# Linear attention into channel mix on one core: q and v loads dealt out anew, one batch turned by TensorE, three by VectorE, a new order

## The chip, the core and the metric

The kernel runs on one core of one Trainium2 chip. The metric is device time in microseconds of one execution; the median of three executions counts. The engines are TensorE (PE, its weight loads PEld), VectorE (DVE), ScalarE (ACT), GpSimd (POOL) and SyncE (SP); SP, ACT and POOL also issue DMAs.

## What is computed

Two stages, one behind the other. For 4 batches of 4 heads, 1088 tokens and head size 32, q and k are projected on two sketches of 8 rows; the outer product of the two projections (64 features) stands in for the softmax. The result, seen as 1088 x 128 for each batch, goes through a token shift and a squared-ReLU mix with a hidden size of 1024.

```python
def phi(x):
    a = np.einsum('rd,bhsd->bhsr', S1, x)
    b = np.einsum('rd,bhsd->bhsr', S2, x)
    return np.einsum('bhsi,bhsj->bhsij', a, b).reshape(*x.shape[:-1], r * r)
q_p, k_p = (phi(q), phi(k))
kv = np.einsum('bhsf,bhsd->bhfd', k_p, v)
z = np.sum(k_p, axis=2)
num = np.einsum('bhsf,bhfd->bhsd', q_p, kv)
den = np.einsum('bhsf,bhf->bhs', q_p, z)[..., None] + 1e-06
attn_out = num / den
...
x = np.ascontiguousarray(attn_out.transpose(0, 2, 1, 3)).reshape(B, S, H * D)
...
xk = mu_k * x + (1.0 - mu_k) * x_prev
xr = mu_r * x + (1.0 - mu_r) * x_prev
k = np.maximum(xk @ w_k, 0.0)
v = k * k @ w_v
r = 1.0 / (1.0 + np.exp(-(xr @ w_r)))
return r * v
```

## The kernel before

Everything stays in on-chip memory between the stages. The program is a list of small tasks, written out by hand in the string `ORDER`: each entry is a function's name, its numbers (a batch, a half or a group), the engine (A, V, G, S for ACT, DVE, POOL, SP) and, behind @, the banks of PSUM that it writes. Each engine runs its own instructions in exactly that order and waits at an instruction until what it needs is there. `LOADS` lists the input loads and the engine that issues each, in the same way (`k01@S` is the second piece of batch 0's k, issued by SP; w0, w1, w2 are the three weights); eight semaphores (called DMAHW0 to DMAHW7) are shared out among the DMAs of SP and ACT, and a DMA that takes a semaphore again waits until the DMA that had it has landed.

The tasks of the attention of a batch b, in the order of need:

- `kturn` (DVE, two halves) transposes k in blocks of 32; `kproj` (PE) projects it; `abev` copies the projections out of PSUM (tile `ab`), and `kp` multiplies them to features.
- `zmm`, `zev`, `wmm`, `wsq` sum the features of k, send the sum back through the sketch and put it beside the query's sketch (tile `SQ`), so that one product with q gives the features and the denominator together.
- `qturn` (DVE) transposes q, `abw` (PE) projects it with `SQ`, `abwev` copies it out; `pw`, `dred`, `drec` make the reciprocal of the denominator, `an` scales one factor with it, `qp` (DVE) forms the query's 64 features.
- `kvmm` (PE) forms the state from `kp` and v, `kvev`, `kdmm`, `kvcp` bring it into place.
- The query's features must be transposed once more before they meet the state. The set `TURNED` says how: a batch in it is turned by TensorE (`qtt`, `qt`: 17 transposes through PSUM, copied out by `qttev` and `qtev`, then `xt` and `xmh`), the others by one block transpose of VectorE (`qf`), followed by `xmm` with 32 x 32 tiles of the array.
- `xev`, `xtev` copy the result out (tile `X`), `xs` puts the token before in front, `xk` and `xkt` form the mixed input `XK` in bf16, `xb` a bf16 copy for the gate.

The second stage runs in nine groups g of rows (0 to 7: a half batch, 512 rows, of batch g // 2; 8: the last 64 of each batch, 256 rows). `f1.g.c` (PE, two matmuls) makes a quarter of the hidden values, `relu` and `sq` work on it on ACT, DVE or POOL, `f2` multiplies it with the second weight; `rr` and `sig` form the gate, `fin` (DVE) the output tile `osb`, `st` stores it. `wkc`, `wvc`, `wrc` (POOL) convert the weights, and `wkc` and `wrc` scale them with the mixing factors that `wmu` (DVE, six small instructions) derives from the product `mumm` (PE) of `mu_row`. `zz.n` are n products of zeros, 128 x 128 by 512 columns, whose result nobody reads.

Before the change, batches 0 and 1 are in `TURNED`, and the attention is worked through in the order 0, 1, 3, 2. All loads of q, k, v and the weights are issued by SP; a batch's v comes in four pieces of 32 rows, two for the rows of the tile's lower half (`v00`, `v01`) and two for the upper half (`v02`, `v03`). The lines that the change touches first:

```python
qin = [const.tile([P, U * D], F32, name=f"q{b}") for b in range(B)]
...
s = v[b].rearrange("h (a y t) d -> y a h t d", y=2, t=17)[y, :, :, 9 * z:9 * z + m, :]
e.dma_start(vin[b][64 * y + z:64 * y + 64:2, :, :m, :].rearrange("p h m d -> p h (m d)"),
            s.rearrange("a h m d -> a h (m d)"))
```

## Time and profile before

| what | value |
|---|---|
| median of three executions | 90.34 us (90.07 to 90.85) |
| the profiled execution, in all | 89.4 us |
| its span, from the first to the last instruction | 87.6 us |
| busy time in the span | PE 74.5, DVE 64.7, ACT 58.6, POOL 57.0 us |
| DMA | 10.27 MB, of it 7.80 MB read |

The profile is that of one execution; its span leaves out 1.8 us that lie around it. PE, DVE, ACT and POOL are listed with the time in which they worked; a share near 100% in a stretch says that the engine had little to wait for there. "[0.74 <-DVE ZL L206]" behind an instruction says that its engine stood idle for 0.74 us before it, until DVE's instruction of line 206 on tile ZL was done.

### The profile page before, as it was taken

To read this page: it belongs to the slowest core of one execution; us is meant where nothing else is said; L and a number is where in the kernel's file an instruction comes from. 1 tells how busy PE (TensorE), PEld (TensorE's weight loads), DVE (VectorE), ACT (ScalarE), POOL (GpSimd) and SP (SyncE) were. 2 spreads that over 40 slices of the span, in tenths; PEclk is the share of its full clock that TensorE was granted. 3 is DMA by queue.
4 is the path that set the end of the run, shared out by engine and by line. 5 is a ranking of instruction groups with operands and counts; after the bars stand their busy time and mean duration, and the time that the engine had idled before them with its cause. 6 is when DMAs were issued, how large, how long until landed. Compare 5 with 4: busy or idle time off the path is not lost.

```text
span 87.6 us, 3769 instructions
## 1 busy us (share of the span) xinstructions
PE 74.5 (85%) x1655; PEld 54.4 (62%) x1655; DVE 64.7 (74%) x105; ACT 58.6 (67%) x86; POOL 57.0 (65%) x73
## 2 busy tenths in 40 slices
...
GB/s 29 332 245 199 265 391 204 218 260 388 419 216 200 153 75 11 0 7 0 36 90 6 7 0 4 7 15 90 74 68 19 58 69 42 66 3 39 137 218 30
DMA packets 6732, 10.27 MB, mean 117 GB/s; under 512 B 746, under 2 KB 4044, under 8 KB 6716
## 3 DMA queue, kind: packets, MB, share of 16 engines
...
q8 instruction: 13, 0.21, 1.1%
q10 hardware_dynamic: 228, 0.23, 0.9%
q0 software_dynamic: 96, 0.16, 0.7%
q14 instruction: 3, 0.02, 0.1%
HBM read 7.80 MB, written 2.23 MB: 115 GB/s over the span
## 4 chain that ended last, share of the span: by engine, by line
PE 45%; DMA 26%; DVE 15%; POOL 4%; issue 4%; ACT 1%; POOLq 1%; SPq 1%; ACTq 0%
DMA v<-in_v_dram 17%; PE ps L536 12%; PE ps L568 11%; DMA k<-in_k_dram 9%; DVE XK L515 4%; PE ps L437 3%; PE ps L365 3%; PE ps L265 3%; PE ps L581 3%; DVE qp L248 3%; DVE qf L427 3%; PE ps L495 2%; PE ps L483 2%; DVE osb L591 1%; DVE X L243 1%
## 5 line engine op out<-in xcount | busy, mean ns | idle before, releaser
L544 ACT ACTIVATE k<-ps 128x1024 bf16<-128x1024 f32 (+1 forms) x30 | 28.0, 969 | 3.4 <-PE ps L536 3.1
L248 POOL TENSOR_TENSOR k<-k 128x1024 bf16<-128x1024 bf16 x11 | 21.5, 1970 | 6.0 <-ACT k L544 3.6
L536 PE MATMUL ps<-XK,wk 128*128 128x512 bf16 (+1 forms) x72 | 19.3, 368 | 0.6 <-DVE XK L515 0.4
L568 PE MATMUL ps<-wv,k 128*128 128x128 bf16 x272 | 19.3, 219 | 0.3 <-ACT k L544 0.3
L568 PEld LDWEIGHTS <-k 128*128 128x128 bf16 x272 | 16.9, 98 | 3.6 <-issue 0.6
L248 POOL TENSOR_TENSOR kp<-ab 128x1024 f32<-128x1024 f32 (+1 forms) x8 | 17.4, 2175 | 1.7 <-ACT ab L241 1.5
L556 ACT ACTIVATE k<-k 128x1024 bf16<-128x1024 bf16 (+1 forms) x12 | 11.9, 1021 | 0.1
L248 DVE TENSOR_TENSOR qp<-an,ps 128x1152 f32<-128x1152 f32 (+1 forms) x8 | 10.1, 1281 | 0.6 <-POOL an L248 0.5
L255 DVE STREAM_TRANSPOSE kT<-k 128x576 f32<-128x576 f32 x8 | 6.1, 771 | 5.1 <-DMA k<-in_k_dram 5.1
L536 PEld LDWEIGHTS <-wk 128*128 128x128 bf16 x72 | 5.7, 97 | 4.8 <-DVE XK L515 1.5
L248 DVE TENSOR_TENSOR k<-k 128x1024 bf16<-128x1024 bf16 (+1 forms) x13 | 7.7, 644 | 0.4 <-PE ps L568 0.4
L346 DVE STREAM_TRANSPOSE qT<-q 128x1088 f32<-128x1088 f32 x4 | 5.2, 1305 | 3.6 <-DMA q<-in_q_dram 3.6
L365 PE MATMUL ps<-SQ,qT 128*32 128x96 f32 x256 | 7.4, 276 | 0.0
L265 PEld LDWEIGHTS ps<-SK,kT 128*32 128x32 f32 x288 | 5.5, 125 | 3.0 <-issue 2.2
L265 PE MATMUL ps<-SK,kT 128*32 128x64 f32 x288 | 7.0, 245 | 0.4 <-issue 0.2
L546 DVE TENSOR_SCALAR k<-ps 128x1024 bf16<-128x1024 f32 x6 | 7.2, 1214 | 0.0
L241 ACT COPY abw<-ps 128x256 f32<-128x256 f32 (+1 forms) x7 | 2.7, 385 | 6.2 <-PE ps L365 6.2
L365 PEld LDWEIGHTS ps<-SQ,qT 128*32 128x32 f32 x256 | 6.5, 126 | 0.4 <-issue 0.4
L591 DVE TENSOR_TENSOR osb<-ps,r 128x512 f32<-128x512 f32 (+1 forms) x9 | 5.8, 650 | 1.2 <-DMA out_dram<-osb 1.2
L322 PEld LDWEIGHTS ps<-kp,v 128*32 128x32 f32 x288 | 4.7, 110 | 2.1 <-issue 1.3
L248 POOL TENSOR_TENSOR an<-abw,den 128x144 f32<-128x144 f32 (+2 forms) x6 | 3.0, 501 | 4.3 <-DVE den L405 4.0
L322 PE MATMUL ps<-kp,v 128*32 128x64 f32 x288 | 5.7, 221 | 0.0
...
## 6 DMA issues: line engine op xcount, KB each, us to landing
k<-in_k_dram SPq DMA_DIRECT2D x8, 272.0 KB, 5.6
...
```

Of the source, the lines that this page charges most:

```text
L248: (nc.vector if eng == "V" else nc.gpsimd).tensor_mul(o, a, b)
L255: nc.vector.transpose(_ap(sb["kT", b][:, 0, 64 * y:], [[1, 2], [P, 9], [2, 32]]), kin[b][:, y].rearrange("p (z m d) -> p z m d", z=2, m=9))
L265: nc.tensor.matmul(_ap(d, [[n, 2], [1, 32]]), sb["kT", b][:, m, 32 * c:32 * c + 32], SK[:].rearrange("p x h r -> p x (h r)"), skip_group_c ...
L322: nc.tensor.matmul(o[32 * h:32 * h + 32, :F], vin[b][:, h, m, :], sb["kp", b, j][:, 4 * (m - KG[j][0]) + h].rearrange("p i j -> p (i j)"), ...
L346: nc.vector.transpose(sb["qT", b][:, u0:u1, :].rearrange("p u a -> p (u a)"), qin[b][:, u0 * D:u1 * D])
L365: nc.tensor.matmul(o[32 * c:32 * c + 32, n:n + 96], sb["qT", b][:, 16 * g + 4 * t + c, :], SQ[b][:].rearrange("p h r -> p (h r)"), skip_gr ...
L536: nc.tensor.matmul(h[:, c, :], wk[:, P * (2 * cp + c):P * (2 * cp + c) + P], x, skip_group_check=True)
L544: nc.scalar.activation(o, h, RELU)
L546: nc.vector.tensor_relu(o, h)
L556: nc.scalar.activation(o, i, SQUARE)
L568: nc.tensor.matmul(o[:, i * P:i * P + P], k2[:, i * P:i * P + P], wv[:, 2 * cp + c, :], start=(cp == 0 and c == 0 and i == 0), stop=(cp == ...
L591: nc.vector.tensor_mul(o[:].rearrange("p i f -> p (i f)")[:, :n], ps["o", g][:, :n], sb["r", g][:, :n])
```

## The change

1. `TURNED` is {0}: batch 1 is turned by VectorE like 2 and 3.
2. The tile of q gets a gap of four numbers in its middle, so that each row of q is loaded as two runs of 2176 bytes in place of one of 4352; `qturn` reads around the gap.
3. The pieces of v are issued in the order lower, upper, lower, upper half, and two of batch 0's four pieces by ACT. The loads of `mu_row` stay behind the loads of `LOADS` in the program and so stand behind those two pieces in ACT's queue.
4. `ORDER` is new from end to end: the attention goes 0, 2, 1, 3, the second stage's groups in the order 0, 1, 4, 5, 3 and 2, 8, 6, 7; there are 12 products of zeros in place of 7; `mumm` stands ahead of `kproj` of batch 0 and `wmu` some 20 tasks later; several copies, ReLUs and squares change their engine.

```diff
-TURNED = {0, 1}
+TURNED = {0}
...
-k00@S k01@S q0@S v00@S v01@S v02@S v03@S w0@S k10@S k11@S q1@S w1@S v10@S v11@S v12@S v13@S w2@S k20@S k21@S q2@S
-k30@S k31@S q3@S v20@S v21@S v22@S v23@S v30@S v31@S v32@S v33@S
+k00@S k01@S q0@S v00@S v02@A v01@S v03@A w0@S k10@S k11@S q1@S w1@S v10@S v12@S v11@S v13@S w2@S k20@S k21@S q2@S
+k30@S k31@S q3@S v20@S v22@S v21@S v23@S v30@S v32@S v31@S v33@S
...
-kturn.0.0 zz.6@0 smm@0 kturn.0.1 sev zz.1@0 kproj.0.1@0 sqc.1 qturn.0 sqc.0 sqc.3 kproj.0.0@1 abev.0.1.A sqc.2
+kturn.0.0 zz.7@0 smm@0 kturn.0.1 mumm@1 sev zz.1@0 kproj.0.1@0 sqc.0 qturn.0 sqc.1 sqc.3 kproj.0.0@2 abev.0.1.A
...
-    qin = [const.tile([P, U * D], F32, name=f"q{b}") for b in range(B)]
+    qin = [const.tile([P, 2, U // 2 * D + 4], F32, name=f"q{b}") for b in range(B)]
...
-            y = slice(n * int(name[2]), n * int(name[2]) + n) if len(name) > 2 else slice(0, 2 * n)
-            e.dma_start(qin[b][:, y], q[b].rearrange("h (a u) d -> (h a) (u d)", u=U)[:, y])
+            y = slice(int(name[2]), int(name[2]) + 1) if len(name) > 2 else slice(0, 2)
+            e.dma_start(qin[b][:, y, :n], q[b].rearrange("h (a y u) d -> (h a) y (u d)", y=2, u=U // 2)[:, y])
...
-    def qturn(b, part=2):
+    def qturn(b):
...
-        u0, u1 = ((0, 16), (16, U), (0, U), (0, 17), (17, U))[part]
-        nc.vector.transpose(sb["qT", b][:, u0:u1, :].rearrange("p u a -> p (u a)"), qin[b][:, u0 * D:u1 * D])
+        nc.vector.transpose(sb["qT", b][:].rearrange("p (y u) a -> p y (u a)", y=2), qin[b][:, :, :U // 2 * D])
```

The order of instructions at the three places that matter below. Names are those of the tiles; in brackets are the semaphores that the instruction waits for, DMAHW those of loads, the others those of an engine. Lines of the changed kernel are one or two lower than those of the one before.

PE at the start of the program, before: from the first product that needs a load to batch 0's `abw` (L354).

```order
L199 MATMUL ps<-ident,S_67 32x16 [waits DMAHW2_49,DMAHW0_49,Pool_49]
L201 MATMUL ps<-S_67,ez 128x32 [waits DVE_49]
L185 MATMUL ps<-zero 128x512 [waits DVE_49]
L265 MATMUL ps<-SK,kT 32x2x32 x36
L213 MATMUL ps<-ident,mu_row 128x2 [waits DMAHW5_49,DMAHW4_49,Activation_49]
L301 MATMUL ps<-ab_231 32x32 [waits Activation_49]
L309 MATMUL ps<-zs,ZL 128x32 [waits Activation_49]
L354 MATMUL ps<-SQ_160,qT 32x48 [waits DVE_49,Pool_49]
```

The same stretch after the change.

```order
L198 MATMUL ps<-ident,S_67 32x16 [waits DMAHW2_49,DMAHW0_49,Pool_49]
L200 MATMUL ps<-S_67,ez 128x32 [waits DVE_49]
L212 MATMUL ps<-ident,mu_row 128x2 [waits DMAHW3_49,DMAHW1_49]
L184 MATMUL ps<-zero 128x512 [waits DVE_49]
L264 MATMUL ps<-SK,kT 32x2x32 x36
L184 MATMUL ps<-zero 128x512 [waits Activation_49]
L300 MATMUL ps<-ab_231 32x32 [waits Activation_49]
L308 MATMUL ps<-zs,ZL 128x32 [waits DVE_49]
L184 MATMUL ps<-zero 128x512 [waits DVE_49]
L352 MATMUL ps<-SQ_160,qT 32x48 [waits Pool_49]
```

The product with `mu_row` has moved ahead of all of batch 0's k products (L265, now L264), and zeros stand around `zmm` (L301, now L300) and behind `wmm` (L309, now L308).

ACT's queue at the start, before.

```order
L154 DMA S_67<-in_S_dram 8x32
L155 DMA S_67<-in_S_dram 8x32
L168 DMA mu_row<-in_moe_mu_k_dram 1x128
L169 DMA mu_row<-in_moe_mu_r_dram 1x128
L170 ACT_TABLE_LOAD
L170 ACTIVATE warm<-warm 8x1 [waits DVE_49]
```

ACT's queue after the change.

```order
L153 DMA S_67<-in_S_dram 8x32
L154 DMA S_67<-in_S_dram 8x32
L148 DMA v_76<-in_v_dram 32x4x288 [waits Pool_49]
L148 DMA v_76<-in_v_dram 32x4x256
L167 DMA mu_row<-in_moe_mu_k_dram 1x128 [waits DMAHW1_49]
L168 DMA mu_row<-in_moe_mu_r_dram 1x128 [waits DMAHW3_49]
L169 ACT_TABLE_LOAD
```

The two loads of `mu_row` now stand behind two pieces of v, and each waits for a load that has landed: DMAHW1 and DMAHW3 are the semaphores for which DVE's two `kturn` of batch 0 wait, those of `k00` and `k01`. On SP, `k10` waits for `q0`, where before it waited for the first load of `mu_row`.

DVE in the middle, before: from batch 1's `wsq` (it writes tile SQ_161) to the first `qp` of batch 1.

```order
L313 TENSOR_TENSOR SQ_161<-ps,m_150 128x4x8 [waits PE_49]
L243 COPY ab_540<-ps 128x320 [waits PE_49]
L346 STREAM_TRANSPOSE qT<-q_74 128x1088 [waits DMAHW7_49]
L243 COPY ab_587<-ps 128x256 [waits PE_49]
L243 COPY abw<-ps 128x18x16 [waits PE_49,Activation_49]
L546 TENSOR_SCALAR k_506<-ps 128x1024 [waits PE_49]
L400 TENSOR_REDUCE den<-pw_113 128x18 [waits Pool_49]
L405 RECIPROCAL den<-den 128x18 [waits DVE_49]
L400 TENSOR_REDUCE den<-pw_113 128x16 [waits Pool_49]
L405 RECIPROCAL den<-den 128x16 [waits DVE_49]
L248 TENSOR_TENSOR qp<-an,ps 128x1152 [waits Pool_49]
```

DVE in the middle after the change: from the `wsq` of batches 2 and 1 to batch 2's `qf`.

```order
L312 TENSOR_TENSOR SQ_162<-ps,m_150 128x4x8 [waits PE_49]
L312 TENSOR_TENSOR SQ_161<-ps,m_150 128x4x8 [waits Activation_49]
L344 STREAM_TRANSPOSE qT<-q_73 128x1088
L242 COPY abw<-ps 128x18x16 [waits PE_49,Activation_49]
L247 TENSOR_TENSOR k_542<-k_472 128x1024
L247 TENSOR_TENSOR pw_112<-abw 128x34x8 [waits DVE_49,Activation_49]
L398 TENSOR_REDUCE den<-pw_112 128x34 [waits DVE_49]
L254 STREAM_TRANSPOSE kT<-k_71 128x2x9x32 [waits DMAHW1_49]
L247 TENSOR_TENSOR qp<-an,ps 128x1152 [waits Pool_49]
L247 TENSOR_TENSOR qp<-an,ps 128x1024 [waits PE_49]
L425 STREAM_TRANSPOSE qf<-qp 128x2176 [waits DVE_49]
```

A batch that VectorE turns has moved forward: its `qp` is followed at once by the block transpose `qf` (L425) on the same engine, where before batch 1 went to TensorE.

More of the change, by code (lines that the diff above doesn't have):

```diff
@@ L36 @@
-kp.0.1.G mumm@0 abev.0.0.A wmu zmm.0@7 zev.0.A wmm.0 kp.0.0.G wsq.0 abw.0.0@7 kturn.1.0 abw.0.1@0 abwev.0.0.A
-kturn.1.1 abwev.0.1.A pw.0.0.V kvmm.0.0@1 dred.0.0.V pw.0.1.G drec.0.0 kproj.1.0@2 dred.0.1.V an.0.0.G drec.0.1
-kvmm.0.1 qp.0.0 an.0.1.G abev.1.0.A wkc.G kproj.1.1@3 kvev.0.A kdmm.0 abev.1.1.A qp.0.1 qtt.0@7 kp.1.0.G qt.0.0@56
-kvcp.0.A qttev.0.A qturn.1 qt.0.1@01 qtev.0.0.A xt.0 qtev.0.1.A kturn.2.0 xmh.0.0@6 wrc xtev.0.V kturn.2.1 xs.0
-xmh.0.1@0 xev.0.0.A kp.1.1.G xk.0.0 kvmm.1.0@1 xev.0.1.A f1.0.2@56 kturn.3.0 zmm.1@2 wvc.G relu.0.2.A kvmm.1.1 xk.0.1
@@ L41 @@
-f1.0.0@34 xb.0.G kturn.3.1 kvev.1.A f1.1.2@56 zev.1.A relu.0.0.A kdmm.1 xkt.0 wmm.1 kproj.3.0@0 kvcp.1.V wsq.1
-sq.0.2.G relu.1.2.A f1.1.3@12 abev.3.0.V f1.0.3@34 qturn.2 kproj.3.1@0 relu.1.3.A abw.1.0@5 kp.3.0.G sq.0.0.A
-abev.3.1.V f1.0.1@67 abwev.1.0.V abw.1.1@0 relu.0.3.A relu.0.1.V rr.0@1 pw.1.0.G abwev.1.1.A f2.0.0@2 sq.0.1.A
-dred.1.0.V pw.1.1.G zmm.3@6 drec.1.0 f1.1.0@34 dred.1.1.V an.1.0.G kproj.2.1@7 drec.1.1 sq.0.3.A zev.3.V an.1.1.G
-qp.1.0 f2.0.1 sq.1.2.G f2.0.2 sig.0 wmm.3 f2.0.3 relu.1.0.A wsq.3 qturn.3 rr.1@1 qt.1.0@56 sq.1.3.G sq.1.0.A
```

45 lines of the change are left out of this document (27 added, 18 removed).

## The prediction

> **What bounds the kernel now.** I read the page's busy times first, then the busy times in windows, then the chain of work that ended last, then the timeline of the first 16 us, where the chain and the change meet. The page's first rows, and the window from the first product of the second stage (24.98 us) to PE's end:
>
> ```profile
> span 87.6 us, 3769 instructions
> PE 74.5 (85%) x1655; PEld 54.4 (62%) x1655; DVE 64.7 (74%) x105; ACT 58.6 (67%) x86; POOL 57.0 (65%) x73
> 24.98:82.31 57.33, 55.98 (x1248) 41.22 (x1246) 48.73 (x72) 50.63 (x70) 41.59 (x40) 1.00 0.21 49
> ```
>
> The columns of the window are its length, then PE, PEld, DVE, ACT, POOL, the granted clock, the DMA share and GB/s. So there are two stretches. From 25 us on PE works 56.0 of 57.3 us and is the bound; ACT (50.6) and DVE (48.7) are not far behind. Before 25 us PE mostly waits, for loads and for batch 0's chain. What the changed PE work costs can be read from pieces of the chain, which count issue time:
>
> ```profile
> 38.30 0.11 PE ps L450
> 39.95 0.24 PE ps L460 x8
> 40.74 0.99 PE ps L495 x8
> 41.73 1.02 PE ps L483 x8
> 52.27 1.47 PE ps L437 x41
> 53.74 0.28 PE ps L444 x16
> ```
>
> The first stretch, from the timeline (start, duration, in brackets the wait before it):
>
> ```profile
> 1.37 0.29 ACTq L155 DMA_DIRECT2D S<-in_S_dram  x1
> 1.99 0.27 ACTq L169 DMA_DIRECT2D mu_row<-in_moe_mu_r_dram  x1
> 3.67 1.44 DVE L255 STREAM_TRANSPOSE kT<-k 128x576 f32<-128x576 f32 x2 [1.17 <-DMA k<-in_k_dram]
> 3.86 0.30 PE L199 MATMUL ps<-ident,S 16*32 16x16 f32 x8
> 5.47 0.58 PE L185 MATMUL ps<-zero 128*128 128x512 bf16 x1 [0.74 <-DVE ZL L206]
> 5.98 2.15 PE L265 MATMUL ps<-SK,kT 128*32 128x64 f32 x72
> 8.06 0.58 PE L213 MATMUL ps<-ident,mu_row 2*128 2x2 f32 x2
> 8.67 0.53 PE L301 MATMUL ps<-ab 128*32 128x32 f32 x18
> 9.00 1.31 DVE L346 STREAM_TRANSPOSE qT<-q 128x1088 f32<-128x1088 f32 x1 [3.59 <-DMA q<-in_q_dram]
> 9.48 0.64 PE L309 MATMUL ps<-zs,ZL 128*128 128x32 f32 x2 [0.27 <-ACT zs L241]
> 10.65 1.26 DVE L219 TENSOR_TENSOR omu<-omu,tmp 128x1 f32<-128x1 f32 x1
> 12.55 0.39 PE L354 MATMUL ps<-SQ,qT 128*32 128x48 f32 x8 [2.43 <-DVE SQ L313]
> 12.69 2.73 PE L365 MATMUL ps<-SQ,qT 128*32 128x96 f32 x64
> 24.98 0.59 PE L536 MATMUL ps<-XK,wk 128*128 128x512 bf16 x2
> 38.45 1.50 PE L365 MATMUL ps<-SQ,qT 128*32 128x96 f32 x64
> ```
>
> Batch 0's chain runs through it: `kproj` starts at 5.98, its sum is ready at 10.1 (9.48 + 0.64), but `abw` starts only at 12.55, since DVE has `wmu` (10.2 to 12.3, of it 1.26 in L219) ahead of `wsq`. `abw` ends at 15.4, and the first `f1` starts 9.6 us after that.
>
> **The change, part by part.** *Batch 1 on VectorE.* PE loses 16 transposes (2 x 1.02), 2 x 0.99 of `xmh`, 0.24 and 0.11, in all 4.4, and gains `xmm` (1.47 + 0.28) and a second `kdmm` transpose (0.1): 2.5 us less on the engine that bounds. DVE pays for it:
>
> ```profile
> L427 DVE STREAM_TRANSPOSE qf<-qp 128x2176 f32<-128x2176 f32 x2 | 4.9, 2440 | 0.0
> L515 DVE SCALAR_TENSOR_TENSOR XK<-X,rat 128x1088 bf16<-128x1088 f32 x2 | 2.7, 1348 | 0.5 <-POOL X L508 0.5
> L248 DVE TENSOR_TENSOR qp<-an,ps 128x1152 f32<-128x1152 f32 (+1 forms) x8 | 10.1, 1281 | 0.6 <-POOL an L248 0.5
> L346 DVE STREAM_TRANSPOSE qT<-q 128x1088 f32<-128x1088 f32 x4 | 5.2, 1305 | 3.6 <-DMA q<-in_q_dram 3.6
> L546 DVE TENSOR_SCALAR k<-ps 128x1024 bf16<-128x1024 f32 x6 | 7.2, 1214 | 0.0
> ```
>
> One `qf` more is 2.44. One `qturn` (1.31) now stands behind the first `f1`, and copies, squares and reductions that change their engine come to about 1.0 on DVE when added up by their rows, ReLUs given to ACT (2 x 1.21) taken off. DVE's work from the first `f1` on goes from 48.7 to about 53.5; PE's falls to 56.0 - 2.5 = 53.5 by the window. So the two are level, and the longest engine has no less than 53.5: the saving on PE can't pay in full.
>
> *The start.* `wmu` leaves the way of `wsq`: worth up to 12.2 - 10.2 = 2.0. But `mumm` now stands ahead of `kproj`, and its load behind two pieces of v and behind `k01`, which has landed by 4.4 (the two kT, 0.72 apart). So the load is issued by about 4.7. How long it takes, no row shows; before, it had landed when `mumm` came at 8.06. The shortest like it: S, issued by 1.66, was there by 3.86, 2.2 us. The longest: a piece of v, by the tile's row.
>
> ```profile
> DMA to landing us min/median/max: 4.9/7.5/7.7
> ```
>
> The loads by window (the last two columns are the DMA share and GB/s), and three rows that the next parts need:
>
> ```profile
> 3.00:5.50 2.50, 1.76 (x14) 0.81 (x12) 1.74 (x4) 0.78 (x2) 0.22 (x2) 1.00 0.90 302
> 11.00:13.00 2.00, 0.45 (x16) 0.48 (x20) 1.33 (x4) 0.00 (x0) 0.90 (x1) 1.00 1.03 394
> 14.00:17.00 3.00, 2.90 (x142) 2.73 (x137) 1.89 (x4) 0.79 (x3) 0.46 (x1) 1.00 1.10 189
> 20.00:24.50 4.50, 3.92 (x57) 2.15 (x58) 3.43 (x6) 2.77 (x4) 3.49 (x5) 1.00 1.03 403
> ...
> 5.51 0.97 SPq L134 DMA_DIRECT2D k<-in_k_dram  x2
> 23.10 0.59 SPq L149 DMA_DIRECT2D v<-in_v_dram  x1
> ...
> k<-in_k_dram SPq DMA_DIRECT2D x8, 272.0 KB, 5.6
> ```
>
> So `mu_row` lands between 6.9 and 12.4. I take 8.1: ahead of it stand q0 and v0, 1.11 MB from about 3.4 on, at the 302 GB/s of the first window 3.7 us, and 1 us to be reported. From there: `mumm` 0.58, a zero product 0.43, `kproj` 2.15, two zeros 0.85, `zmm` 0.53, copy 0.3, `wmm` 0.64, two zeros 0.85 beside `wsq`: `abw` starts at 14.4 in place of 12.55. Its length depends on PE's pace. The granted clock in the rows is 1.00 throughout, yet the same 64 products take 2.73 us at 12.7 and 1.50 at 38.5. With no pause of PE over 0.3 us from 8.1 on, I take the fast pace: `abw` ends at 14.4 + 0.2 + 1.5 = 16.1, 0.7 later than before, and the first `f1` comes at 25.6 (ends: 24.4 with `mu_row` at 6.9; 31.1 with 12.4 and the slow pace).
>
> [...]
>
> *Loads.* The windows show 394 to 403 GB/s while k, q and the first weight move and 189 while v does, so v's 2.2 MB take some 11 us. If pieces for two halves ran side by side they would take 5.6; if not, 11. I take no gain: behind 25.6 the first that waits for a load is `kvmm` of batch 2, at 31.9 in the layout below; the last piece of v2, issued by 23.7 before, is there 7.5 us later, at 31.2. So loads are just covered, and what is late there is DVE. The q runs of 2176 bytes are as long as k's, which move at the same 400 GB/s: nothing. `k10` is issued after q0 has landed (9.0, by `qturn`'s wait, for 5.5 before); with the 5.6 us that k's loads take it is there at 14.6, before the 16 us at which `kproj` of batch 1 needs it.
>
> [...]
>
> *From the first `f1` to the last `fin`.* I lay the new order out on DVE, each instruction by its row. From 25.5: q transposes 2 x 1.31, ReLU 1.21, `qp` 2.56, `qf` 2.44 and thirteen small ones of 0.16 to 0.77, 5.9 together: batch 2's `qf` ends at 40.2, without a gap. Then `xmm` 1.8 on PE, copies out and `xk` 1.35, behind POOL's `xs`: 45.1. Batch 1: `qp`, `qf` to 50.1, `xmm` to 52.7 (it waits 0.8 for ACT's ReLU to free two banks), `xk` done at 55.9. Batch 3: four small ones and two squares 2.7, `an` 0.55, `qp`, `qf` to 64.1, `xmm` to 66.0, `xk` done at 69.4. What is left is level on PE, DVE and ACT, 12 to 13 us each; the last `fin` ends at 82.8. That is 57.2 us from the first `f1`; before it was 59.05, to 84.03.
>
> *The end.*
>
> ```profile
> 83.61 0.42 DVE L591 TENSOR_TENSOR osb<-ps,r 128x256 f32<-128x256 f32 x1 [1.19 <-DMA out_dram<-osb]
> ```
>
> The 1.19 us for which the last `fin` waited for a buffer go, since group 8 no longer comes last; they are inside the 57.2. The last stores are twice as large and one stands behind two others on SP: 3.7 us to the span's end, for 3.57 before.
>
> Sum: 82.8 + 3.7 = 86.5 for a span of 87.6: -1.1 us. The profiled execution is 0.9 us under the median; taken off the median, 90.34 - 1.1 = 89.2 us.
>
> **Rivals.** *The wait for `mu_row` decides.* For: it is the only load whose product blocks all of PE. Against: before, it landed by 8.06 with little ahead of it. Each us of landing after 8.1 is one at the end; from 10.1 on the kernel is more than 1% slower, at 10.2 it is 91.3 us, at 12.4 with the slow pace 94.7.
>
> *The start comes early.* `mu_row` at 6.9 and halves side by side: first `f1` at 24.4, batch 2's loads no longer close: 88.0 us. The rows of S speak for it, the 189 GB/s against.
>
> *DVE becomes the bound with gaps.* Before, DVE stood idle for 59.05 - (48.7 + 0.5) = 9.8 us on the way; my layout leaves 3.7. With 5 us of gaps it is 90.5, with 7 us 92.5. For: an order laid out by hand shows too few waits, each engine being about 90% full. Against: DVE now has work of four batches to choose from.
>
> The halves of v doing nothing is inside the forecast.
>
> **How the numbers follow.** Forecast 0.42, `mu_row` late 0.20, early start 0.20, DVE with gaps 0.18. About 1%, 0.9 us, is what a measurement of this kernel can tell from no change. The forecast is 0.2 beyond that, so its chance splits 0.25 faster, 0.16 same, 0.01 slower; late: 0.05 same, 0.15 slower; early: 0.19 faster, 0.01 same; gaps: 0.02 faster, 0.09 same, 0.07 slower. Faster 0.46, same 0.31, slower 0.23. The range goes from 87.2 (early start with a us less of waits) to 92.0 (`mu_row` at 10.9, or 6.5 us of gaps).
>
> **What would show it.** In the changed profile: the start of batch 0's `kproj` and what PE waits for before it (8.1 + 1.0 here); `abw`'s 64 products at 1.5 or 2.7; the first `f1` at 25.6; GB/s while v moves, near 190 or near 400; the ends of `qf` at 40.2, 50.1, 64.1; DVE's busy time from the first `f1` (53.5); no wait for `osb`. The forecast is wrong if PE's chain is full again while DVE has gaps of over 5 us, or if `kproj` starts after 11.

## The result, and the profile after

The changed kernel is slower: 95.98 us median (95.61 to 97.97) against 90.2 us (89.98 to 90.85) for the kernel before, a ratio of 1.061 with a 95% interval of 1.053 to 1.070. On another chip it came to 96.04 us and 1.071 (1.062 to 1.080). The forecast was 89.2 with a range to 92.0. Ratios with an interval leave disturbed executions out; where too few were left, the median and the spread of all executions stand instead.

The profiled execution took 96.29 us, of it 94.5 in the span. From its page: the span, the busy times, the clock granted to PE in 40 slices of 2.36 us, and the queue that brings in program code (packets, MB, share).

```profile
span 94.5 us, 3883 instructions
PE 73.6 (78%) x1716; PEld 53.2 (56%) x1716; DVE 69.3 (73%) x106; ACT 58.5 (62%) x84; POOL 52.2 (55%) x65
PEclk9996558999999999999999999999965999999997
q8 instruction: 13, 0.21, 0.9%
```

PE has 0.9 us less work than before (73.6 for 74.5) and DVE 4.6 more, but no engine fills the longer span: the time went into waits. The timeline of the changed kernel up to the first `f1` shows the first of them; the last row is that `f1`.

```profile
4.32 0.23 ACTq L168 DMA_DIRECT2D mu_row<-in_moe_mu_r_dram  x1
8.65 1.31 DVE L344 STREAM_TRANSPOSE qT<-q 128x1088 f32<-128x1088 f32 x1 [3.24 <-DMA q<-in_q_dram]
10.55 0.55 PE L212 MATMUL ps<-ident,mu_row 2*128 2x2 f32 x2 [5.62 <-DMA mu_row<-in_moe_mu_r_dram]
11.57 2.15 PE L264 MATMUL ps<-SK,kT 128*32 128x64 f32 x72
16.73 1.50 PE L363 MATMUL ps<-SQ,qT 128*32 128x96 f32 x64
25.16 0.27 PE L481 MATMUL ps<-ident,qp 128*128 128x128 f32 x1 [1.91 <-issue]
28.22 0.61 PE L534 MATMUL ps<-XK,wk 128*128 128x512 bf16 x2
```

PE stands 5.62 us for `mu_row`; `kproj` starts at 11.57 in place of 5.98 before. The chain of waits of the changed kernel (start, duration, what) has these pieces that answer to nothing in the chain before:

```profile
4.32 6.09 DMA mu_row<-in_moe_mu_r_dram
...
23.25 1.91 issue
...
44.98 1.50 issue
...
62.23 2.06 DVE an L247
...
72.76 0.83 POOL XB L244
73.59 0.25 POOL XBT L244
```

"issue" is time in which PE waited for nothing that the profile names. DVE's timeline of the changed kernel gives the ends of `qf` (start plus duration) and of `xk` for batches 2, 1 and 3, and batch 3's copies ahead of its `xk`:

```profile
39.97 2.44 DVE L425 STREAM_TRANSPOSE qf<-qp 128x2176 f32<-128x2176 f32 x1
46.07 1.60 DVE L513 SCALAR_TENSOR_TENSOR XK<-X,rat 128x1088 bf16<-128x1088 f32 x1
50.09 2.44 DVE L425 STREAM_TRANSPOSE qf<-qp 128x2176 f32<-128x2176 f32 x1
58.47 1.35 DVE L513 SCALAR_TENSOR_TENSOR XK<-X,rat 128x1088 bf16<-128x1088 f32 x1
66.82 2.45 DVE L425 STREAM_TRANSPOSE qf<-qp 128x2176 f32<-128x2176 f32 x1
...
73.86 1.20 DVE L242 COPY X<-ps 64x64 f32<-64x64 f32 x3 [2.22 <-POOL XBT L244]
75.16 1.60 DVE L513 SCALAR_TENSOR_TENSOR XK<-X,rat 128x1088 bf16<-128x1088 f32 x1
```

With the last `fin` at 90.44 the misses line up stretch by stretch:

| stretch | forecast us | measured us | miss |
|---|---|---|---|
| start to first `f1` | 25.6 | 28.22 | +2.6 |
| to the end of batch 2's `qf` | 14.6 | 14.19 | -0.4 |
| to batch 2's `xk` | 4.9 | 5.26 | +0.4 |
| to batch 1's `qf` | 5.0 | 4.86 | -0.1 |
| to batch 1's `xk` | 5.8 | 7.29 | +1.5 |
| to batch 3's `qf` | 8.2 | 9.45 | +1.2 |
| to batch 3's `xk` | 5.3 | 7.49 | +2.2 |
| to the last `fin` | 13.4 | 13.68 | +0.3 |
| to the span's end | 3.7 | 4.06 | +0.4 |
| sum | 86.5 | 94.5 | +8.0 |

Windows of the changed kernel (length, PE, PEld, DVE, ACT, POOL, granted clock, DMA share, GB/s); the fourth is the whole stretch from the first `f1` to the last `fin`:

```profile
8.50:14.50 6.00, 3.95 (x77) 2.64 (x77) 1.31 (x1) 0.80 (x2) 1.32 (x1) 0.50 0.95 282
15.00:19.00 4.00, 3.07 (x111) 2.40 (x110) 2.52 (x7) 0.77 (x2) 2.48 (x2) 1.00 1.14 263
69.50:72.50 3.00, 3.00 (x101) 2.19 (x102) 2.14 (x4) 1.04 (x2) 0.00 (x0) 0.50 0.13 12
28.22:90.44 62.22, 55.26 (x1308) 41.92 (x1302) 54.91 (x73) 50.90 (x70) 39.05 (x35) 0.97 0.12 36
```

That stretch is 62.22 us, for 59.05 before and 57.2 forecast. DVE works 54.9 of it (53.5 forecast) and stands 7.3 (3.7 forecast): 1.4 and 3.6 too much, the 5.0 us of the miss.

### The profile page after: what moved, and what is told of

It is laid out like the page before. It is cut to its first block, busy times and chain, and to the rows that moved or that the text cites. A ratio compares the mean times of both kernels' runs of the same rounds, so it can differ in the third digit from the quotient of the medians.

```text
span 94.5 us, 3883 instructions
## 1 busy us (share of the span) xinstructions
PE 73.6 (78%) x1716; PEld 53.2 (56%) x1716; DVE 69.3 (73%) x106; ACT 58.5 (62%) x84; POOL 52.2 (55%) x65
## 4 chain that ended last, share of the span: by engine, by line
PE 48%; DVE 19%; issue 12%; DMA 10%; POOL 3%; ACT 3%; POOLq 1%; SPq 0%; DVEq 0%
PE ps L534 8%; DMA mu_row<-in_moe_mu_r_dram 6%; PE ps L264 6%; PE ps L435 5%; PE ps L321 5%; PE ps L566 5%; PE ps L363 4%; DMA k<-in_k_dram 3%; DVE XK L513 3%; DVE k L247 3%; DVE qp L247 3%; DVE qf L425 3%; DVE X L242 2%; PE ps L184 2%; DVE an L247 2%
## 5 line engine op out<-in xcount | busy, mean ns | idle before, releaser
L542 ACT ACTIVATE k<-ps 128x1024 bf16<-128x1024 f32 (+1 forms) x31 | 29.4, 984 | 2.5 <-PE ps L534 1.5
L247 POOL TENSOR_TENSOR kp<-ab 128x1024 f32<-128x1024 f32 (+1 forms) x8 | 17.3, 2176 | 7.6 <-ACT ab L240 7.6
L247 POOL TENSOR_TENSOR k<-k 128x1024 bf16<-128x1024 bf16 (+1 forms) x10 | 17.4, 1759 | 7.2 <-ACT k L542 4.2
L554 ACT ACTIVATE k<-k 128x1024 bf16<-128x1024 bf16 x12 | 12.5, 1058 | 1.9 <-PE ps L566 1.8
L244 POOL CAST XB<-X 128x288 bf16<-128x288 f32 (+1 forms) x8 | 6.9, 889 | 6.0 <-ACT X L240 4.9
L247 DVE TENSOR_TENSOR k<-k 128x1024 bf16<-128x1024 bf16 (+1 forms) x14 | 9.5, 716 | 0.1
L240 ACT COPY ab<-ps 128x320 f32<-128x320 f32 (+1 forms) x7 | 2.8, 404 | 9.0 <-PE ps L264 9.0
L425 DVE STREAM_TRANSPOSE qf<-qp 128x2176 f32<-128x2176 f32 x3 | 7.3, 2445 | 0.1
L435 PE MATMUL ps<-qf,kvr 32*32 32x256 f32 x192 | 5.6, 466 | 1.8 <-DVE qf L425 1.8
L584 ACT ACTIVATE r<-ps 128x512 f32<-128x512 f32 (+1 forms) x9 | 5.1, 574 | 2.8 <-PE ps L579 2.8
L184 PE MATMUL ps<-zero 128*128 128x512 bf16 x12 | 5.4, 584 | 1.5 <-DVE warm L152 1.2
L264 PE MATMUL ps<-SK,kT 128*32 128x64 f32 x288 | 6.5, 244 | 0.0
L264 PEld LDWEIGHTS ps<-SK,kT 128*32 128x32 f32 x288 | 5.4, 126 | 1.9 <-issue 1.4
```

The lines of the kernel that those rows point to most:

```text
L184: nc.tensor.matmul(PS[:, banks[0], :], zero[:, :P], zero[:], skip_group_check=True)
L244: nc.gpsimd.tensor_copy(o, i)
L247: (nc.vector if eng == "V" else nc.gpsimd).tensor_mul(o, a, b)
L264: nc.tensor.matmul(_ap(d, [[n, 2], [1, 32]]), sb["kT", b][:, m, 32 * c:32 * c + 32], SK[:].rearrange("p x h r -> p x (h r)"), skip_group_c ...
L425: nc.vector.transpose(sb["qf", b][:, s0:s1].rearrange("p s f a -> p (s f a)"), sb["qp", b][:, s0:s1].rearrange("p s i j -> p (s i j)"))
L435: nc.tensor.matmul(o[c][32 * h:32 * h + 32, :32 * T], kv[32 * c:32 * c + 32, f, h, :], _ap(r, [[4 * 64, T], [1, 32]]), start=(f == 0), sto ...
```

## The experiments

Each starts from the changed kernel or from one named. The kernel before, run beside them, had medians of 89.6 (e), 90.27 (f), 90.38 (h), 89.67 (i) and 90.63 us (j).

### The wait for mu_row: e1 and e2

e1 puts the two loads of `mu_row` ahead of the loop over `LOADS`:

```diff
+    nc.scalar.dma_start(mu_row[:1, :], moe_mu_k.rearrange("(x d) -> x d", x=1))
+    nc.scalar.dma_start(mu_row[1:, :], moe_mu_r.rearrange("(x d) -> x d", x=1))
     for what in LOADS.split():
         load(what)
```

> The changed kernel, with the two mu_row loads issued on ACT's queue ahead of all other loads but S. Theory: the wait of PE for mu_row (5.62 us, landing at 10.41) is what puts the first f1 at 28.22 in place of 25.6, and everything behind it is shifted with it. Then mu_row is there before 6.5, batch 0's kproj starts at about 6, the first f1 at 25.0 to 25.6, and the time is 92.5 to 93.6 us. Rival: the order from the first f1 on is held by something that does not move with the start (loads of batch 2, or DVE). Then the first f1 comes earlier but the time stays above 94.8.

e2 leaves the loads and moves the product:

```diff
-kturn.0.0 zz.7@0 smm@0 kturn.0.1 mumm@1 sev zz.1@0
+kturn.0.0 zz.7@0 smm@0 kturn.0.1 sev zz.1@0
...
-abw.0.1@2
+abw.0.1@2 mumm@1
```

> The changed kernel, its loads untouched, with mumm moved on PE from ahead of kproj to behind batch 0's abw. Nothing that waits for mu_row then stands ahead of batch 0's chain, though the load itself stays as late as before. Theory (mu_row only matters because its product blocks PE): kproj at about 6, first f1 at 23.5 to 25.5, time 91.5 to 93.6. Rival (what is late is the loads as a whole, v and q of batch 0 behind each other on the queues): kproj early, but qturn or kvmm of batch 0 waits, first f1 after 26.5, time above 94.

Measured: e1 93.54 us (91.81 to 94.02), first `f1` 22.90; e2 91.21 us, ratio to before 1.024 (1.011 to 1.037), first `f1` 23.03. Timeline of e2: `kproj`, `abw` and the first `f1`; then its window from there to the last `fin`.

```profile
6.19 2.15 PE L264 MATMUL ps<-SK,kT 128*32 128x64 f32 x72
11.52 1.50 PE L363 MATMUL ps<-SQ,qT 128*32 128x96 f32 x64
23.03 1.04 PE L534 MATMUL ps<-XK,wk 128*128 128x512 bf16 x4
```

```profile
23.03:85.13 62.10, 54.62 (x1306) 41.30 (x1302) 55.00 (x73) 50.95 (x69) 38.63 (x35) 1.00 0.22 59
```

The load is issued as late in e2 as in the changed kernel (4.15 for 4.32); only its product no longer stands in front. Both theories held in direction: the first `f1` came earlier than either had it (25.0 to 25.6 in e1, 23.5 to 25.5 in e2), and e2's time is 0.3 us under its range. In e2 the first `f1` comes 5.2 us earlier, the stretch behind it keeps its length (62.10 for 62.22), and the profiled span falls from 94.5 to 89.2. So in these two profiles the start passes through to the end whole. By the ratios to before (1.061 and 1.071, now 1.024) it is worth 3.3 to 4.2 us. Either way the wait for `mu_row` is the largest single loss. e1 gains as much at the start but is 64.56 us from the first `f1` to the last `fin`; it has 3.3 us of the gaps that the section on PE shows, and half clock from 34.33 to 37.74. e2 is still slower than before by 2.4%: its `f1` is 2 us earlier than before, so the stretch behind it is what loses.

### Batch 3's chain on DVE: f2, e3, f3, h2

f2, from e2: `an.3.2.V` becomes `an.3.2.G`.

> The kernel of e2_mumm_behind with one multiplication of batch 3 (an, 128x272) on POOL in place of DVE, ahead of POOL's square sq.5.3. In e2 it takes 2.12 us on DVE while POOL runs a square that began just before; on POOL the same shape took 0.66. [...] Rival: the square then stands behind an, f2 of group 5 comes later and PE's xmm with it: less than 0.5 us gained.

The estimate was that `an` is slow on DVE because of POOL's square beside it, and that the time falls by 1.2 to 1.7 us, to 89.5 to 90.1. Measured: 89.57 us, ratio 0.984 (0.969 to 0.999). POOL's and DVE's timeline of f2:

```profile
57.17 0.91 POOL L247 TENSOR_TENSOR an<-abw,den 128x272 f32<-128x272 f32 x1 [3.91 <-ACT k L542]
58.04 5.59 POOL L247 TENSOR_TENSOR k<-k 128x1024 bf16<-128x1024 bf16 x3
58.11 2.48 DVE L247 TENSOR_TENSOR qp<-an,ps 128x1152 f32<-128x1152 f32 x2 [0.54 <-POOL an L247]
60.63 2.44 DVE L425 STREAM_TRANSPOSE qf<-qp 128x2176 f32<-128x2176 f32 x1
```

`an` takes 0.91 on POOL and 2.06 on DVE beside a square of POOL (the changed kernel's chain, above); batch 3's `qf` ends at 63.07 for 64.90 in e2, and the stretch from the first `f1` to the last `fin` is 60.11 for 62.10. The time lies within the estimate. Another product of the same shape, `pw` of batch 3, took 0.44 on DVE in the changed kernel while POOL stood idle. So a product of this shape on DVE was seen at 0.44 with POOL idle and at 2.06 beside POOL's square; what holds it there no run shows.

e3, from the changed kernel, moves `xb.1.G` from behind `xev.3.0.A` to behind `xk.1.2`; f3, from e2, moves it to just ahead of `xmm.3`.

> The changed kernel with one task moved: xb.1 (POOL's copy of batch 1's X to XB) stands right behind xk of batch 1 in place of behind xev.3.0 of batch 3. Batches 1 and 3 share one half of X32, so in the changed kernel the later part of XB for batch 1 is read from columns that batch 3 has begun to overwrite, and POOL's copy stands between the two halves of batch 3's copies out (POOL waits 4.5 us for ACT, then DVE waits 2.2 us for POOL). Here batch 1's own columns are copied. Theory: batch 3's xk ends 1.2 to 1.8 us earlier and so does the kernel: 94.2 to 94.8. Rival: the end hangs on ACT, DVE and PE, which are level there, and xk of batch 3 is not what they wait for: 95.5 to 96.2.

> The kernel of e2_mumm_behind with xb.1 (POOL's copy of batch 1's X into XB) put ahead of batch 3's xmm in program order; on POOL it stands where it stood, behind sq.2.0, but copies batch 1's own columns and waits for nothing of batch 3. Theory: POOL does it at 64 to 66 in place of 67.5 to 68.5, DVE's copies of batch 3 wait for PE and ACT alone, xk of batch 3 ends 0.8 to 1.3 us earlier and the time falls by as much: 89.9 to 90.5. Rival: the copy now runs beside qf on DVE and slows it, as it did with DVE's squares in e3_xb1_early, or the end hangs on ACT and PE: 91 or more.

e3: 97.33 us (94.47 to 98.17), a miss by the median; the profiled execution is the one of 98.17, so what follows is that execution's. From `qf` to `xk` of batch 3 it is 6.38 us for 7.49, as the theory had it, but the stretch before is 11.3 us for 9.45. DVE's timeline of e3, where POOL's copy (59.74 to 62.7) and its squares now run beside batch 3's chain:

```profile
61.24 1.30 DVE L247 TENSOR_TENSOR k<-k 128x1024 bf16<-128x1024 bf16 x1
62.46 0.52 DVE L247 TENSOR_TENSOR pw<-abw 128x272 f32<-128x272 f32 x1
63.81 1.75 DVE L247 TENSOR_TENSOR k<-k 128x1024 bf16<-128x1024 bf16 x1
65.49 2.13 DVE L247 TENSOR_TENSOR an<-abw,den 128x272 f32<-128x272 f32 x1
```

The two squares took 0.69 and 0.63 in the changed kernel. So in this execution the copy moved its cost from a wait to DVE's instructions. f3: 90.49 us, 1.002 (0.993 to 1.010), against 1.024 for e2. In its profile DVE's copies start 0.7 us after `xmm`'s end, for 1.8 in e2; but `xmm` itself ran at half clock and took 0.9 back, so they start at 68.50 for 68.55. So the times have the theory's direction, and the one profile doesn't show the gain.

The place of `xb.1` is not only a matter of time. Batches 1 and 3 use the same half of tile X, and in the changed kernel's order `xb.1` stands behind `xev.3.0`, which writes two of every four blocks of columns. POOL's copy waits for just that write:

```profile
72.76 0.83 POOL L244 CAST XB<-X 128x768 bf16<-128x768 f32 x1 [4.52 <-ACT X L240]
```

So 512 of the 1056 columns of batch 1's copy for the gate hold batch 3's values; the changed kernel and the runs that keep this place (e1, e2, e4, f1, f2, f4, h4, i0) compute that part of the gate from the wrong batch. Before, and in e3, f3, h2, h3, i1, i2 and j2, the copy stands ahead of that write. The copies are equally large either way, so the times can be compared.

h2 is e2 with both, `an.3.2.G` and f3's place of `xb.1.G`.

> The changed kernel with three tasks moved: mumm behind batch 0's abw (e2), an of batch 3 on POOL (f2), xb.1 ahead of batch 3's xmm (f3). Theory (the three losses are separate and add up): first f1 at 23.0, 59.2 to 59.8 us from there to the last fin, span 86.3 to 87, time 88.0 to 88.8, a ratio to before of 0.97 to 0.982. Rival (they overlap: what an and xb.1 free is waited away at the next place, since PE, DVE and ACT are level): no better than f2 alone, a ratio of 0.983 or more.

Its profile has 59.70 us from the first `f1` (22.95) to the last `fin` and a span of 86.7, where the theory had 59.2 to 59.8 and 86.3 to 87; the executions scatter (89.49, 87.17 to 92.70), so the sum holds in the profile and is not settled by the times.

### PE standing still for nothing visible: h4, i1, i3

The gaps marked "issue" have places that don't change. Counted along PE's instructions in each trace they stand ahead of the 449th, 705th, 961st and so on, every 256th, within two (in the changed kernel 0.52 us ahead of the 450th, 1.91 of the 706th, 0.28 of the 1730th, 1.50 of the 1987th). Queue q8 brings the program in 13 packets of 0.21 MB in all, 16 KB each. In the trace of f4 (below) a packet ends at 20.00, 27.84 and 33.88 and PE goes on at 21.25, 29.33 and 35.32, 1.2 to 1.5 us later; in the changed kernel at 23.59 and 25.16. A packet doesn't start long ahead: in the 17 traces without the wide products of i1 to i3, the packet for the 705th instruction starts 1.0 to 6.0 us after PE has passed the 449th, and takes 1.0 to 1.5 us. So a gap opens where PE is through its 256 instructions before the next packet is there. h4 puts 16 small products ahead, in PE's wait for `mu_row`:

```diff
+        for i in range(16 if n == 7 else 0):
+            nc.tensor.matmul(PS[:, banks[0], :32], zero[:, :P], zero[:, :32], skip_group_check=True)
```

> The changed kernel with 16 small zero products (128x32) more on PE in the first 5 us, where PE waits for mu_row anyway: 32 more PE instructions ahead of everything else. In the traces so far PE stands still with no visible cause ahead of the same instructions each time, and counted along PE's instructions these are the 449th, 705th, 961st, 1217th, 1473rd, 1729th and 1985th, 256 apart. Theory (PE waits there for the next piece of its program): the gaps stay at those numbers, so they move 32 instructions back in the program: none ahead of the last of batch 0's 16 transposes (1.91 us there in the changed kernel), one ahead of the first of them at most, where PE waits for qp anyway. Rival (the gap belongs to that transpose, its bank or its operand): it stays ahead of the last transpose. For the time: first f1 at 27.3 to 28.3, time 95 to 96.

PE's timeline of h4:

```profile
24.14 0.37 PE L450 MATMUL ps<-ident,qp 128*128 128x128 f32 x1 [4.02 <-issue]
44.35 0.65 PE L323 MATMUL ps<-kp,v 128*32 128x64 f32 x30 [0.30 <-issue]
49.22 0.29 PE L444 MATMUL ps<-qf,kvr 32*32 32x32 f32 x6 [2.03 <-issue]
```

The theory held: the gap left the last transpose (L481 in the changed kernel) and stands at the same count, now ahead of the first one, L450. It also grew, to 3.25 us behind a wait for `qp` (4.02 in all), and half clock was recorded from 22.00 to 28.82; the first `f1` came at 31.05, and the time was 99.69 us (95.19 to 100.11), worse than the theory's 95 to 96.

i1 (from h2) and i3 (from h1, below) use `kprojw` and `abww`, functions that both kernels have: one product with 128 columns of weights for four with 32.

> The kernel of h2_three with kproj and abw written in products of 128 columns of weights in place of four of 32 (the same sums in a quarter of the instructions; functions that both kernels have and do not use): about 800 PE instructions fewer of some 3450, most of them in the first 40 us. Theory (PE stands still because its program comes in pieces of 256 instructions that arrive late while loads run): fewer pieces are needed while loads run, there are fewer than 0.5 us of such gaps and the runs lie closer together: 87.3 to 88.6 us, a ratio to before of 0.965 to 0.98. Rival (the gaps come from something else, or the wide products run slower since the four narrow ones work side by side): first f1 later than 23.3, ratio 0.985 or more.

> The kernel of h1_before_wmu (before, with wmu behind qp of batch 0) with kproj and abw in wide products. In h1 abw started at 10.6 as expected and batch 0's qf was ready 1.5 us earlier than before, but PE then stood 2.46 us ahead of its 705th instruction. Theory (the piece of PE's program was late): with fewer instructions the gap is gone, the first f1 comes at 22.8 to 23.8, ratio to before 0.975 to 0.985. Rival (something else holds PE there): first f1 after 24.5, ratio 0.99 or more.

i1 96.41 us, 1.067 (1.059 to 1.075); i3 95.86 us, 1.060 (1.048 to 1.072). Of i1: the packets of code; its window at the start; the groups of the wide products; then the same groups of h2.

```profile
q8 instruction: 10, 0.16, 0.8%
```

```profile
8.00:24.00 16.00, 15.01 (x147) 12.78 (x147) 8.10 (x19) 2.43 (x7) 7.78 (x7) 0.50 1.05 322
```

```profile
L274 PE MATMUL ps<-SK,kT 128*128 128x64 f32 x72 | 11.4, 317 | 0.0
L374 PE MATMUL ps<-SQ,qT 128*128 128x96 f32 x64 | 9.9, 316 | 0.0
```

```profile
L264 PE MATMUL ps<-SK,kT 128*32 128x64 f32 x288 | 7.1, 245 | 0.8 <-DVE kT L254 0.8
L363 PE MATMUL ps<-SQ,qT 128*32 128x96 f32 x256 | 6.2, 246 | 0.0
```

Both halves of the expectation came true, the wrong one larger. No gap is left at any 256th instruction, in i1 or in i3; with h4 and the packets' times this shows that the gaps are the program's arrival. But the wide products cost 21.3 us for 13.3, in part because PE stays at half clock to 24 us, though it works 15 of 16. At full clock, too, one wide product costs more than the four narrow ones that it replaces: batch 3's `abw` takes 2.02 us in i1 and 1.50 in h2, its `kproj` 2.33 and 1.48.

### The loads, through the back door: f4, h1, j1, j2

f4 is e2 with the two lines of `LOADS` of before.

> The kernel of e2_mumm_behind with the loads of v as before: in the old order (both pieces of one half one after the other), all on SP. Theory (alternating the halves gives nothing): GB/s while v moves and the time agree within 0.7 us, 90.6 to 91.8. Rival (the halves run side by side): v moves at a lower rate here, the last load lands 3 us or more later than in e2, and kvmm of batch 2 waits for it: 92.5 or more.

95.91 us (93.2 to 97.06) for 91.21, yet the loads are nearly level: 211 GB/s in the window from 14 to 17 us, 228 in e2, 233 in the changed kernel, 189 before, and the last load's last packet ends at 30.8 us in f4 and 30.6 in e2. The rival's time came without its cause. PE's timeline of f4:

```profile
21.25 0.27 PE L481 MATMUL ps<-ident,qp 128*128 128x128 f32 x1 [2.03 <-issue]
29.33 0.32 PE L300 MATMUL ps<-ab 128*32 128x32 f32 x13 [0.68 <-issue]
35.32 0.89 PE L321 MATMUL ps<-kp,v 128*32 128x64 f32 x39 [1.88 <-issue]
```

In e2 none of the three is there. f4 also has half clock from 22.32 to 25.74 and, on batch 3's `xmm`, from 70.11 to 76.94, and e2 has none in either place. h1 takes the one part of the change that should help into the kernel before:

```diff
-kp.0.1.G mumm@0 abev.0.0.A wmu zmm.0@7
+kp.0.1.G mumm@4 abev.0.0.A zmm.0@7
...
-abev.1.0.A wkc.G kproj.1.1@3
+abev.1.0.A kproj.1.1@3
...
-qp.0.1 qtt.0@7 kp.1.0.G qt.0.0@56
+qp.0.1 wmu qtt.0@7 kp.1.0.G wkc.G qt.0.0@56
```

> The kernel before with one part of the change alone: wmu (six small DVE instructions) moved from ahead of wsq to behind qp of batch 0, with the bank of its product and POOL's wkc moved so that it can stand there. mu_row's load and product stay where they were. Theory (the gain that the forecast saw in the start is real and was buried by mu_row): abw starts near 10.6 in place of 12.55, the first f1 near 23.3 in place of 24.98, and the time is 1.3 to 2 us under before, a ratio of 0.978 to 0.986. Rival: batch 0's chain then waits for wk, whose scaling on POOL now comes later, or for loads, and the first f1 gains under 0.7: 0.992 to 1.005.

91.43 us (89.42 to 91.70) beside 90.38. `abw` starts at 10.6 for 12.55 and batch 0's `qf` is there at 20.98 for 22.51; then PE's timeline of h1 has

```profile
22.63 0.32 PE L460 MATMUL ps<-qtt,kvr 64*32 64x64 f32 x2 [2.46 <-issue]
26.82 0.61 PE L536 MATMUL ps<-XK,wk 128*128 128x512 bf16 x2
```

where the gap before was 0.58. Half clock follows it, from 22.38 to 25.79, in which `xmh` takes 3.6 us for 2.0 before; so batch 0's chain lost what it had gained. j1 is h1 with the new `LOADS`, and `mu_row` loaded ahead of them; j2 is h3 (below) with the old.

> The kernel of h1_before_wmu with the loads of the changed kernel (alternating halves, two pieces of v on ACT's queue), the two mu_row loads kept ahead of them on ACT. The five profiles with these loads and an early start (e2, f2, f3, h2, h3) show no gap of PE ahead of its 705th instruction, f4 and h1, with all loads on SP, show 2.0 and 2.5. Theory (with these loads PE's program comes earlier): no such gap over 0.6, first f1 at 22.8 to 23.9, ratio to before 0.973 to 0.985. Rival (its length is chance, or hangs on something else): a gap of 1 to 3 us, first f1 after 24.5, ratio 0.99 to 1.01.

> The kernel of h3_three_no_zeros (the changed kernel with mumm, an of batch 3 and xb.1 moved and without five zero products) with the loads of before: old order, all on SP. The same question from the other side. Theory: the gap ahead of PE's 705th instruction is back with 1 to 2.5 us, the first f1 at 24 to 26 in place of 22.6, the time 90.5 to 94. Rival: no gap, 88 to 89.5 as h3, and f4's 95.9 was something else.

| kernel | queues of v | gap ahead of the 705th us | all such gaps us | first `f1` | `f1` to last `fin` |
|---|---|---|---|---|---|
| before | SP | 0.58 | 0.8 | 24.98 | 59.05 |
| changed | SP, ACT | 1.91 | 4.2 | 28.22 | 62.22 |
| e1 | SP, ACT | 0.40 | 3.7 | 22.90 | 64.56 |
| e2 | SP, ACT | none | 1.7 | 23.03 | 62.10 |
| f4 (e2) | SP | 2.03 | 6.9 | 25.71 | 65.50 |
| h1 | SP | 2.46 | 2.5 | 26.82 | 59.21 |
| j1 (h1) | SP, ACT | 1.32 | 2.9 | 23.29 | 61.29 |
| h3 | SP, ACT | none | 0.2 | 22.61 | 59.58 |
| j2 (h3) | SP | 1.87 | 2.7 | 24.79 | 59.08 |

j2 (91.67 us, 89.78 to 93.20) brings the gap back as the theory had it, in a profiled execution of 89.78. j1 (89.87 us, 0.997, 0.990 to 1.003) is half a hit: `f1` at 23.29, but a gap of 1.32 and another of 1.60 at 27.9, and a ratio that is the rival's. So the new `LOADS` lean towards shorter gaps (f4 against e2, j2 against h3, h1 against j1), though f1_turned, whose program up to there is e2's, had 1.04. The packet's start says it more clearly: for the 705th instruction it came 3.8 to 6.0 us after PE had passed the 449th in the four traces with the old `LOADS`, all on SP, and 1.0 to 3.7 us in the thirteen with the new. For the next piece the two ranges overlap (2.3 to 4.8 and 1.3 to 4.6). What moves the start from run to run within these ranges stays open.

### Batch 1: e4, f1, i2

Batch 1 in `TURNED` again, with `qtt`, `qt`, `qtev`, `xt`, `xmh` in place of `qf.1.2` and `xmm.1`, in the changed kernel (e4), in e2 (f1) and in i1 (i2).

> The changed kernel with batch 1 turned by TensorE again (16 transposes, qtev on ACT, xmh), its tasks in the same stretch of the order, all else as changed; the first f1 stays at 28.2. XB of batch 1 is still copied behind xev.3.0, as in the changed kernel. Theory A (DVE with gaps is the bound behind the first f1, batch 1's qf and xk stand in its chain): faster, 93 to 95. Theory B (PE's time counts, as the forecast took it): slower by the 2.5 us that PE gets back, 97 to 98.5. In between: PE and DVE are level and the turn of batch 1 is worth nothing by itself.

> The kernel of e2_mumm_behind (mumm behind batch 0's abw), with batch 1 turned by TensorE again: 16 transposes, qtev on ACT, xmh, in place of qf on VectorE and xmm. Measured with the start repaired, so that only the stretch from the first f1 (23.0) to the last fin (85.1, 62.1 us) differs. Theory A (DVE in its order, with 55 us of work and 7 us of gaps, is the bound): DVE has 3 to 4 us less, the stretch shortens to 59 to 60.5, time 88.5 to 90 where e2 has 91.2. Theory B (PE's time counts, as the forecast took it): the stretch grows by up to 2.5 us, time 92 to 94.

> The kernel of i1_wide with batch 1 turned by TensorE again (as in f1_turned). It is the one comparison of the change's main part without the gaps of PE's program and without the late mu_row. Theory A (DVE in its order is the bound behind the first f1): DVE has 3 to 4 us less, the stretch from the first f1 to the last fin is 1.5 us or more shorter than in i1_wide. Theory B (PE counts): it is 1.5 to 2.5 us longer. Theory C, by the two profiles of f1 and e2 with their gaps taken off (60.1 and 60.4): level within 1 us, moving the turn of a batch between the two engines is worth nothing, since the one's gain is the other's loss.

e4 97.15 us (94.44 to 99.57); f1 94.02 us, 1.024 (1.005 to 1.042), where e2 had 1.024; i2 101.72 us, 1.138 (1.132 to 1.144), where i1 had 1.067. From the first `f1` to the last `fin`, in windows of f1, then i1, then i2:

```profile
23.39:89.27 65.88, 57.19 (x1253) 42.16 (x1246) 51.19 (x73) 53.63 (x73) 38.90 (x35) 1.00 0.19 50
```

```profile
28.73:89.36 60.63, 56.42 (x1082) 44.44 (x1081) 53.12 (x72) 51.08 (x69) 40.34 (x36) 1.00 0.11 31
```

```profile
30.71:95.11 64.40, 58.95 (x1026) 45.11 (x1025) 50.54 (x72) 53.53 (x72) 40.44 (x36) 1.00 0.10 29
```

Turned by TensorE, PE and ACT work 2.5 us more each and DVE 2.6 less (i2 against i1), and the stretch is 3.8 us longer; f1 against e2 is 3.8 longer too, of which 2.0 are gaps of PE's program. Theory B held in i2, with more than its 2.5 us, where PE has more to do than in the changed kernel; in f1 it held by the profile and not by the ratio, and e4's times are too far apart to say. So in no run was batch 1 on VectorE the loss. This holds for the one order in which batch 1's tasks were put back; another was not tried.

### The zero products and the control: h3, i0

h3 is h2 without `zz.1`, `zz.2` and `zz.2` behind `zz.7`.

> The kernel of h2_three without the five dense zero products behind the first seven (one ahead of kproj, two ahead of zmm, two ahead of abw). Theory (they keep PE busy and so at its full rate): batch 0's abw takes 2.7 us in place of 1.5, the first f1 comes 0.8 to 1.2 later, and the time is 0.8 to 1.2 us above h2_three. Rival (PE's rate in abw hangs on the seven products before and on kproj): abw at the same pace, and the time within 0.4 us of h2_three.

89.06 us, 0.980 (0.970 to 0.990): in this profile the rival held, `abw` took 1.50 without them. That doesn't settle it: j2, which leaves out the same products, has `abw` at 2.81, and f1_turned, which has them and is e2's program up to there, at 2.57 where e2 has 1.50. That zeros keep PE at its full rate was the author's estimate, and no run shows it. With f2 (0.984, 0.969 to 0.999), h3 is the only kernel here whose interval lies below the kernel before; its gain lies in the start (first `f1` at 22.61 for 24.98).

> The changed kernel itself once more, beside the three below on one chip, so that the runs derived from it have their own measure. Nothing is to be told apart by it alone: if the gaps of PE ahead of its 449th, 705th and every 256th instruction after these have random lengths, the start of the first f1 (28.22 in its first profile) and the time (95.6 to 98) come out with a spread of 2 us or more; if they are fixed, within 0.5 us of the first.

Its profile has the first `f1` at 28.14, `mu_row`'s product at 9.03, a gap of 1.30 ahead of the 705th instruction and `abw` at 2.78: other pieces, the same sum up to there. From the first `f1` to the last `fin` it is 60.98 us for 62.22, without the half clock on batch 3's `xmm`. So two profiles of one kernel can differ by 1.2 us in that stretch, and a smaller difference between two profiles here shows nothing by itself.

## Why the prediction was wrong

- **The load of `mu_row`, mis-sized.** The step "I take 8.1: ahead of it stand q0 and v0 ... and 1 us to be reported" is the first that failed. The 1 us was an estimate that no row gave; from the end of the load's packet to its landing the traces have 0.57 us before (5.02 to 5.59) and 0.61 in the changed kernel (9.80 to 10.41). `mu_row` landed at 10.41, 6.09 us after its issue: 512 bytes behind two pieces of v took nearly as long as a piece of v itself (the tile's row gave 4.9 to 7.7). In the four other profiles with this start (i0, e3, h4, e4) it landed at 8.90 to 9.84, 4.7 to 5.7 us after its issue, so the miss is 0.8 to 2.3 us. The nearest row to a load queued behind v was v's, not S's. From 10.1 on, the text said, the kernel is more than 1% slower, at 10.2 with 91.3 us; that rival came true, and e2 shows its mechanism: without the wait the first `f1` comes 5.2 us earlier.
- **"With no pause of PE over 0.3 us": the start behind it.** `abw` had the fast pace, and its end (18.23) was 2.1 late where `mu_row` was 2.3; the rest of the +2.6 is the gap of 1.91 at 23.25, partly made up elsewhere. In i0 `mu_row` was 0.8 late, `abw` had the slow pace (1.3 more) and the gap was 1.30. That `abw` is fast when PE has no pause was the author's estimate, and no run shows it: this one kernel has both paces (last section). For the gap no term stood in the sum. The profile before had a sign: 0.6 us of "issue" ahead of L460, the 705th instruction there.
- **"I lay the new order out on DVE, each instruction by its row": the layout.** It had 3.7 us of gaps and 53.5 of work; it became 7.3 and 54.9, the third rival's case (92.5 at 7 us). Three places: `an` of batch 3, put down at 0.55, took 2.06 (f2: 1.8 us at `qf`); `xb.1` between the halves of batch 3's copies, which the layout left out (DVE's wait of 2.22 us ahead of these copies, 1.27 in i0; moving it was worth 0.2 to 1.1 us of it, by h2 against f2 and by e3); batch 1's `xmm`, 1.9 us behind `qf` in place of 0.8, since PE had batch 3's `kvmm` and `wmm` ahead of it. Gaps of PE's program add 1.8 in the changed kernel, and half clock on batch 3's `xmm` 0.9 (2.69 us from its first product to its last, for 1.74 in e2). That is not all of it: h3, with `an` and `xb.1` moved and 0.2 us of gaps, still takes 59.58 us where the layout had 57.2. There `qf` to `xk` takes 6.3 us for each of the three batches (4.9, 5.8 and 5.3 in the layout); for batch 2 DVE waits 1.34 us of it for ACT's copy of X. So the way from `qf` to `xk` was laid out too short, and the stretch is no shorter than the 59.05 of before: no run has the time that PE saved. What would bring it out was not tried.
- **The cases were priced as if one excluded the other.** Forecast 89.2, late `mu_row` 91.3, DVE with gaps 92.5: both came. Their excess over the forecast, 2.1 and 3.3, makes 94.6 together, beyond a range that ended at 92.0. (DVE's 1.4 us of extra work is in neither.) Late start and gappy middle have nothing to do with each other, so their sum belonged in the range.
- **Right:** loads gain next to nothing from alternating halves (f4: 211 GB/s for 228); `wmu` out of the way is worth 2 us up to `abw` (h1: 10.6 for 12.55), though h1 and j1 are no faster in the end (`wmu` stands 50 tasks behind `mumm` in the new order, not some 20); PE's saving of 2.5 us of work is real (i2); the tail of 13.4 and the end of 3.7 were 13.68 and 4.06; nothing waited for `osb`. The q runs of 2176 bytes were not tried alone; q0 was turned from 8.65 for 9.00 before.
